# One re-planned kernel: Wq loaded in row halves, halved first-tile chains, doubled VectorE tiles, and 32 short reads of Wqkv on ScalarE's queue

## The chip, the cores and the metric

The kernel runs on one core of one Trainium2 chip. The metric is the device time of the launch in microseconds (us); lower is better. The time before is 184.14 us, the median of three runs (184.11 to 184.27).

## What is computed

One layer block in bf16: a layer norm, then a sliding dilated attention and a gated feed-forward on the same normalised rows, and both are added to the input. S is 2048, D is 512, with 32 heads of 16 values; each position attends to 8 positions, spaced by 2; the hidden width is 1376.

```python
xn = _layernorm(x, axis=-1)
# _A_ref
qkv = (x @ wqkv)                         # 512 -> 3*512
idx = pos[:, None] - off[None, :]        # off = 0, 2, ..., 14
logits = jnp.einsum("bhsd,bhswd->bhsw", q, kg) * scale
attn = _softmax(jnp.where(mask, logits, -1e9), axis=-1)
o = jnp.einsum("bhsw,bhswd->bhsd", attn, vg)   # then o @ wo
# _B_ref
h = _gelu(x @ w_gate) * (x @ w_up)       # then h @ w_down
return x + _A_ref(xn, A_wqkv, A_wo) + _B_ref(xn, B_w_gate, B_w_up, B_w_down)
```

## The kernel before, in words

The 2048 rows are cut into four blocks b = 0..3 of 512 positions, and each block into tiles of 128 rows. Every piece of work is a named task of a small graph (`Graph`, `Task`, `Item`, lines 64 to 382). The task order of each engine is written out by hand in `ORDER` (line 402 on), one list of names for each of TensorE ("pe"), ScalarE ("act"), VectorE ("dve"), GpSimd ("pool") and the DMA queue ("sp"). `schedule` walks these lists only to hand out buffer slots and to find the waits; it has a model of durations (`PARAMS`, `SCHED`, `d_mm`, `d_act`, `d_dve`), which decides which slot a tile gets, and so some of the waits, but does not move a task. An engine works strictly down its list, so a task that waits holds up all that stands behind it.

The stages, with the names that are used below:

- Loads on SP: the first four row tiles (`ld_x0_0` and so on, line 731), Wqkv in three column parts `ld_wq`, `ld_wk`, `ld_wv` (line 687), further row tiles (line 737), then Wg and Wu (`ld_wg0`, `ld_wu0`, line 696), which wait until Wk has landed, and the rest.
- Layer norm: for block 0 on VectorE (`bnst`, `bnag`, `sub`, `rstd`, `norm`; lines 750 to 873) with square roots on ScalarE (`sq`); tile 1 has its sums on ScalarE (`sx1`, `sxx1`, line 760). For later tiles it is on ScalarE. Block 0 is transposed on TensorE (`tpx`, line 899) and evicted by ScalarE and VectorE (`evx`, `evy`); later blocks are transposed by DMA (`trx`, line 882).
- Q, K, V: for block 0, Q and K are made tile by tile (`mma0_0`, `mmt`, line 959: 16 matmuls of 128 columns for each tile), V in four matmul groups of 512 columns (`mm0_2_0_0` to `mm0_2_3_0`, line 1009). For later blocks all twelve groups are 512 wide. ScalarE evicts them (`evq`, `evk`, `evv`, lines 986 and 1020).
- Logits: VectorE multiplies Q by the shifted K for one of four head groups at a time, 4096 elements for each partition (`pr`, line 1040), adds pairs (`pa`, line 1053; a third add only for block 3, `PR_ADD3`), and TensorE sums over the head values with a fixed matrix (`er`, line 1085, 16 matmuls for blocks 0 to 2, 8 for block 3), together with a part of the feed-forward (line 1078).
- Softmax: on VectorE a max over 8 straight from PSUM (`d1`, line 1117), a subtraction in PSUM (`d2`, line 1122), on ScalarE `exp`, then three adds (`d4a` to `d4c`, line 1141), `ln`, `d5`, and the product `d6` (line 1159). The result goes to DRAM (`ss`, line 1168) and comes back replicated to all partitions (`sl`, line 1180).
- Output of attention: VectorE multiplies V by the weights in four parts of 4096 elements (`pv`, line 1188), adds them up (`pw`, line 1197) and folds the sum (`pz`, line 1203).
- Feed-forward: eleven gate and up groups for each block (`fg`, `fu`, lines 1221 and 1260) with gelu and copies on ScalarE (`gelu`, `uev`) and the product on VectorE (`h`, line 1245).
- Down projection and Wo sum in one PSUM tile (`acca`, `accb`, `accd`, `accw`, line 1306); ScalarE evicts (`fe`, line 1339), VectorE adds the input rows (`fin`, lines 1344 and 1350), which were loaded again into XR (`ldxr`, line 1292), and SP stores (line 1357).

TensorE warms up on constants (`warm`, line 678) before the first transpose. PSUM has eight slots in one pool, so TensorE waits for ScalarE where a slot is to be used again.

Of the kernel before, what the change touches and what calls it, by code (L numbers as in the profile page):

```python
# [9 lines left out]
    LAT_X=0.08,  # L10
    LAT_S=0.03,
    TOL=dict(pe=0.6, act=-0.3, dve=0.0, pool=0.0, sp=0.0),
    DMA_ISSUE=0.48,
    DMA_FIXED=2.0,
    DMA_BPUS=330e3,
    ACT_SWITCH=1.35,
    PE_SLACK=0.0,
    PE_MODE_SWITCH=0.115,
    PE_DRAIN=0.2,
    DRAIN=0.1,  # L20
    PE_COLD_F=2.0,
    HAM_TAU=4.0,
    HAM_ENTER=0.52,
    HAM_EXIT=0.30,
)


class PeClock:

    def __init__(self, prm):  # L30
        self.tau = prm["HAM_TAU"]
        self.enter = prm["HAM_ENTER"]
        self.exit = prm["HAM_EXIT"]
        self.f = prm["PE_COLD_F"]
        self.avg = 0.0
        self.t = 0.0
        self.warm = False

    def run(self, start, dur, util):
        import math  # L40
        if start > self.t:
            self.avg *= math.exp(-(start - self.t) / self.tau)
            if self.warm and self.avg < self.exit:
                self.warm = False
            self.t = start
        left = dur
        total = 0.0
        while left > 1e-9:
            step = min(left, 0.2)
            real = step * (1.0 if self.warm else self.f)  # L50
            a = math.exp(-real / self.tau)
            self.avg = self.avg * a + util * (1.0 - a)
            if not self.warm and self.avg > self.enter:
                self.warm = True
            elif self.warm and self.avg < self.exit:
                self.warm = False
            total += real
            left -= step
        self.t = start + total
        return total  # L60

# [36 lines left out]
class Task:  # L98
    def __init__(self, idx, eng, name, dur, emit, prio, table, nbytes, batch, mode=None, latest=None,
# [6 lines left out]
        self.on_act = False  # L106
        self.idx = idx
# [28 lines left out]
class Graph:  # L136
# [70 lines left out]
    def schedule(self, orders, params=None):  # L207
        prm = dict(PARAMS)
        prm.update(params or {})
        LAT_X, LAT_S = prm["LAT_X"], prm["LAT_S"]  # L210
# [12 lines left out]
        efree = dict((e, 0.0) for e in ENGS)  # L223
        act_table = None
        pe_mode = None
        pe_clock = PeClock(prm)
        dma_free = 0.0

        def rdy(t, p, od):
            if p.eng == t.eng and (p.eng == "pe" or od):  # L230
                return p.end
            return p.done + (LAT_S if p.eng == t.eng else LAT_X)

# [33 lines left out]
        for _ in range(len(self.tasks)):  # L267
# [17 lines left out]
            if t.eng == "sp":  # L285
                t.end = est + (t.dur or prm["DMA_ISSUE"])
                t.done = t.end
                if t.nbytes > 0:
                    dma_free = max(t.end, dma_free) + t.nbytes / prm["DMA_BPUS"]
                    t.done = dma_free + prm["DMA_FIXED"]  # L290
            elif t.eng == "pe":
                sw = 0.0
                if t.mode is not None:
                    if pe_mode not in (None, t.mode):
                        sw = prm["PE_MODE_SWITCH"]
                    pe_mode = t.mode
                t.end = est + sw + pe_clock.run(est, t.dur, t.util)
                t.done = t.end + prm["PE_DRAIN"]
            else:
                t.end = est + t.dur  # L300
                t.done = t.end + prm["DRAIN"]
                if t.eng == "act" and t.table is not None:
                    act_table = t.table
# [60 lines left out]
    def emit_engine(self, eng_name, e):  # L364
        if eng_name == "act":
            for t in self.order["sp"]:
                if t.on_act:
                    assert not t.waits
# [20 lines left out]
    def report(self):  # L389
# [16 lines left out]
        "warm0 warm1 warm2 warm3 warm4 warm5 warm6 warm7 warm8 warm9 tpx0_0 warm10 warm11 warm12 warm13 "  # L406
        "warm14 mma0_0 tpx0_1 mmt0_0 mmt0_1 mmt1_0 tpx1_0 mmt1_1 mmt0_2 tpx1_1 mmt1_2 mmt0_3 mmt1_3 "
        "mm0_2_2_0 mm0_2_1_0 fg0_0 mm0_2_0_0 fg0_1 fg0_2 fg0_3 fu0_0 fu0_1 mm0_2_3_0 fg0_4 fu0_2 fu0_3 fu0_4 "
        "fg0_5 mm1_1_0_0 mm1_0_0_0 fu0_5 fg0_6 er0_3 mm1_0_1_0 mm1_1_1_0 fg0_7 mm1_1_3_0 mm1_0_2_0 mm1_2_3_0 "
        "fg1_0 mm1_0_3_0 mm1_1_2_0 fg1_1 fu1_0 fu1_1 fu0_6 fu0_7 fg1_2 fu1_2 mm1_2_2_0 mm1_2_1_0 fg1_3 fu1_3 "  # L410
        "fg0_8 fg1_4 fu0_8 mm1_2_0_0 fg1_5 fg0_9 fu1_4 fu0_9 fu1_5 fg1_6 fg0_10 fu1_6 mm2_0_0_0 mm2_1_0_0 "
        "mm2_1_1_0 mm2_0_2_0 er1_3 fg1_7 mm2_0_3_0 mm2_0_1_0 fg1_8 mm2_1_3_0 mm2_2_0_0 fg2_0 mm2_1_2_0 accd2 "
        "fu1_7 accd1 mm2_2_2_0 fu1_8 acca0 fg1_10 mm2_2_3_0 accb0 fg2_1 fg2_2 accd3 fg2_3 fu2_0 fg1_9 fu2_1 "
        "mm2_2_1_0 fu2_2 fu2_3 er2_3 mm3_1_0_0 mm3_1_3_0 fu1_9 mm3_0_0_0 mm3_1_2_0 mm3_0_2_0 mm3_2_1_0 "
        "mm3_0_1_0 mm3_1_1_0 fg3_0 mm3_0_3_0 fg2_4 mm3_2_0_0 mm3_2_2_0 mm3_2_3_0 fu3_0 fu2_4 fg2_5 fg2_10 "
        "accd7 fu2_5 fg3_1 fu3_1 fg3_2 accd5 acca4 er3_3 fg2_6 accb4 accd6 fu2_6 fg2_7 fg2_8 fg3_10 fu2_7 "
        "fu3_2 fu2_8 fg3_3 fg3_4 fu3_3 fg3_5 fg2_9 fu2_9 fu3_4 fg3_6 fu3_5 fg3_7 fu3_6 fu3_7 fg3_8 fg3_9 "
        "fu3_8 accd11 acca8 accd10 fu3_9 accd9 accb8 acca12 accd13 accd14_0 accd14_1 accw14_0 accw14_1 "
        "accw13 accd15_0 accb12 accw15_0 accw12 accd15_1 accw15_1 accd15_2 accw15_2",
    "act":  # L420
        "c_tbl sx1 sq0 negm1 sxx1 sq1 evx0_0 evx0_1 evq0_0 sq2 evq0_1 evk0_0 evx1_0 sq3 evk0_1 bnst8 evx1_1 "
        "bnst9 evq0_2 evk0_2 evq0_3 evk0_3 ve8 sq6 vp8 sq4 bnag8 evv0_2_0 evv0_1_0 halo1 bnag9 evv0_0_0 va8 "
        "gelu0_0 bnst10 gelu0_2 uev0_0 bnst11 ve10 evv0_3_0 gelu0_1 vp10 gelu0_3 uev0_3 uev0_1 bnag10 "
        "evk1_0_0 evq1_0_0 gelu0_5 bnag11 gelu0_4 uev0_5 uev0_4 uev0_2 vb8 evq1_1_0 evk1_1_0 gelu0_6 gelu0_7 "
        "exp0 sub8 va10 evq1_2_0 vb10 ln0 sub11 d5_0 evk1_3_0 evq1_3_0 evv1_3_0 uev1_0 evk1_2_0 sub9 uev1_1 "
        "uev0_6 uev0_7 gelu1_1 gelu1_0 evv1_1_0 sub10 norm9 uev0_10b gelu1_3 evv1_2_0 gelu0_8 norm10 norm8 "
        "uev1_2 gelu1_2 norm11 gelu1_5 uev1_3 gelu1_4 bnst12 gelu0_9 uev0_9 uev1_5 uev0_8 uev0_10a bnst13 "
        "uev1_6 uev0_10c evv1_0_0 evq2_0_0 gelu0_10 evk2_1_0 ve12 evk2_0_0 vp12 evq2_2_0 bnag12 gelu1_6 "
        "uev1_4 evq2_3_0 gelu1_7 bnag13 evq2_1_0 halo2 evk2_3_0 exp1 bnst14 va12 bnst15 vb12 ve14 evk2_2_0 "
        "vp14 uev1_10b bnag14 ln1 uev1_7 d5_1 sub13 halv1 fe2 bnag15 uev1_8 va14 vb14 sub15 sub12 fe1 "  # L430
        "uev1_10c evv2_2_0 sub14 norm12 norm13 fe0 evv2_3_0 evv2_0_0 gelu2_2 gelu2_1 norm14 fe3 norm15 halo3 "
        "uev1_10a gelu2_0 gelu1_10 uev2_1 evv2_1_0 uev2_0 uev2_3 uev2_2 gelu1_8 uev2_10b uev2_10c gelu2_3 "
        "gelu1_9 evq3_0_0 evk3_0_0 evq3_2_0 evk3_3_0 evk3_2_0 evq3_1_0 exp2 halv2 evk3_1_0 uev1_9 evv3_0_0 "
        "evv3_3_0 ln2 evv3_2_0 evq3_3_0 d5_2 evv3_1_0 uev3_0 halv3 gelu2_5 uev2_10a gelu2_4 uev2_5 uev2_4 "
        "uev3_1 fe5 gelu2_10 gelu3_1 fe7 fe4 uev3_10c gelu3_2 gelu3_0 exp3 uev3_10b uev2_6 uev2_7 fe6 ln3 "
        "uev3_2 d5_3 uev2_8 gelu2_6 uev3_3 gelu2_7 gelu2_9 uev2_9 gelu2_8 gelu3_4 gelu3_5 uev3_5 gelu3_3 "
        "gelu3_6 uev3_6 uev3_4 uev3_7 gelu3_7 fe11 gelu3_10 fe10 gelu3_9 uev3_10a uev3_9 gelu3_8 uev3_8 fe8 "
        "fe9 fe13 fe12",
    "dve":
        "c_wdz bnst0 bnag0 sub0 rstd0 norm0 mean1 sub1 evy0_0 rstd1 norm1 evy0_1 bnst2 bnag2 sub2 rstd2 "  # L440
        "norm2 bnst3 bnag3 sub3 rstd3 norm3 bnst6 bnst4 bnst5 bnst7 bnag6 bnag5 bnag4 bnag7 sub4 sub5 sub6 "
        "sub7 pr0_1 rstd6 rstd4 norm7 norm5 norm6 pr0_0 norm4 pr0_3 pr0_2 pa0_0 pa0_1 pr1_0 mask d1_0 h0_1 "
        "d2_0 pr1_1 h0_2 d4a_0 d4b_0 d4c_0 pa1_0 d6_0 pr1_3 pr1_2 h0_3 rstd8 pa1_1 h0_0 h1_0 rstd10 pv0_1 "
        "pv0_0 pv0_2 pw0_1 h1_1 pv0_3 pw0_2 h0_4 d1_1 pw0_3 d2_1 pz0 h0_10 pr2_0 d4a_1 pr2_1 d4b_1 d4c_1 "
        "pr2_2 d6_1 pr2_3 pa2_0 rstd12 pa2_1 h1_3 fin2 h1_2 pv1_0 rstd14 pv1_2 pv1_3 pv1_1 h1_10 pw1_1 d1_2 "
        "pw1_2 d2_2 pw1_3 pr3_0 d4a_2 pz1 d4b_2 h1_4 d4c_2 pr3_2 pr3_3 fin1 d6_2 pr3_1 h2_0 pa3_0 pa3_1 fin0 "
        "h2_1 pa3_2 pv2_1 d1_3 h2_10 d2_3 fin3 pv2_0 h2_2 d4a_3 pv2_2 d4b_3 h3_0 d4c_3 pw2_1 d6_3 pw2_2 fin7 "
        "pv2_3 h2_3 pw2_3 h2_4 fin6 pz2 pv3_1 pv3_2 fin4 pv3_0 pv3_3 h3_2 fin11 h3_3 fin5 pw3_1 h3_1 h3_10 "
        "h3_4 fin10 pw3_2 fin8 pw3_3 fin9 pz3 fin14_0 fin14_1 fin13 fin15_0 fin15_1 fin12 fin15_2",
# [15 lines left out]
def d_mm(n, cnt=1):  # L465
    return cnt * max(64, n) * 0.4213e-3


def d_act(n):
    return 0.10 + 0.00085 * n  # L470
# [950 lines left out]
```

## Time and profile before, and how to read it

| what | value |
|---|---|
| median of 3 runs | 184.14 us (184.11 to 184.27) |
| profiled execution: span from first to last instruction | 182.8 us |
| median less the span (launch and end, around the instructions) | 1.3 us |
| busy: TensorE, VectorE, ScalarE | 178.0 us (97%), 168.8 us (92%), 129.3 us (71%) |
| mean granted TensorE clock | 0.999 |
| DMA: bytes and share of 16 engines | 19.44 MB, 36.3% |
| first Wg matmul, last matmul's end | 17.17 us, 180.28 us |

The profiled execution's own time is its span and the 1.3 us around it. "PE" is TensorE's matmuls, "PEld" its weight loads, "DVE" VectorE, "ACT" ScalarE, "POOL" GpSimd, "SPq" the queue of DMA issues. A group's line gives busy time, mean ns of one instruction, and the idle time of the engine just before it, with what ended it. Durations of neighbours on one engine overlap in part: four matmuls of 128x512 are recorded with 379 ns each but follow each other 0.86 us for four, and two VectorE products of 4096 elements, recorded with 2287 ns each, take 4.49 us together. For a sum over a chain the distance from start to start is the right measure.

### The profile page before, as it was taken

To read this page: it belongs to the slowest core of one execution; us is meant where nothing else is said; L and a number is where in the kernel's file an instruction comes from. 1 tells how busy PE (TensorE), PEld (TensorE's weight loads), DVE (VectorE), ACT (ScalarE), POOL (GpSimd) and SP (SyncE) were. 2 spreads that over 40 slices of the span, in tenths; PEclk is the share of its full clock that TensorE was granted. 3 is DMA by queue.
4 is the path that set the end of the run, shared out by engine and by line. 5 is a ranking of instruction groups with operands and counts; after the bars stand their busy time and mean duration, and the time that the engine had idled before them with its cause. 6 is when DMAs were issued, how large, how long until landed. Compare 5 with 4: busy or idle time off the path is not lost.

```text
span 182.8 us, 2777 instructions
## 1 busy us (share of the span) xinstructions
PE 178.0 (97%) x1060; PEld 89.8 (49%) x1060; DVE 168.8 (92%) x169; ACT 129.3 (71%) x266; POOL 11.1 (6%) x23
## 2 busy tenths in 40 slices
PE   8799999999999999999999999999999999999994
PEld 2685444554444544444444555444444444444673
DVE  3769999999999999999999989999999999999932
ACT  5589977899899899869997596934396764145011
POOL 6000000104000000504000000000000000000000
PEclk9999999999999999999999999999999999999999
DMA  4999559610364000002742000136310246222333
GB/s 111 359 376 377 132 113 299 211 50 21 97 190 98 0 0 0 4 14 74 201 115 61 0 0 0 37 81 158 129 59 0 46 138 221 57 84 74 91 106 107
DMA packets 26220, 19.60 MB, mean 107 GB/s; under 512 B 13824, under 2 KB 23008, under 8 KB 26208
## 3 DMA queue, kind: packets, MB, share of 16 engines
q1 hardware_dynamic: 26208, 19.44, 36.3%
q8 instruction: 8, 0.13, 0.3%
q14 instruction: 4, 0.03, 0.1%
HBM read 14.71 MB, written 3.15 MB: 98 GB/s over the span
## 4 chain that ended last, share of the span: by engine, by line
PE 89%; DMA 8%; SPq 1%; issue 0%; DVE 0%; DVEq 0%
PE PS L1221 38%; PE PS L1306 28%; PE PS L1009 18%; DMA Wg<-in_B_w_gate_dram 5%; DMA Wqkv<-in_A_wqkv_dram 3%; PE PS L1260 2%; PE PS L1085 2%; PE PS L1078 1%; SPq L731 1%; SPq L687 0%; DVE OB L1350 0%; DVEq L376 0%
## 5 line engine op out<-in xcount | busy, mean ns | idle before, releaser
L1306 PE MATMUL PS<-Wd,HT 128*128 128x512 bf16 (+2 forms) x209 | 40.8, 345 | 0.0
L1221 PE MATMUL PS<-xnT,Wg 128*128 128x512 bf16 x160 | 39.6, 379 | 0.3 <-DMA Wg<-in_B_w_gate_dram 0.3
L1221 PE MATMUL PS<-xnT,Wu 128*128 128x512 bf16 x160 | 38.8, 379 | 0.0
L1009 PE MATMUL PS<-xnT,Wqkv 128*128 128x512 bf16 x160 | 37.8, 379 | 0.0
L1040 DVE TENSOR_TENSOR UNI<-QT,KT 128x4096 f16<-128x4096 bf16 x16 | 36.4, 2287 | 0.1
L1188 DVE TENSOR_TENSOR UNI<-VN,PT 128x4096 f16<-128x4096 bf16 x16 | 36.0, 2286 | 0.0
L1306 PEld LDWEIGHTS PS<-Wd,HT 128*128 128x128 bf16 x209 | 19.7, 98 | 19.0
L1238 ACT ACTIVATE UU<-PS 128x512 bf16<-128x512 f32 x40 | 22.8, 604 | 7.9 <-PE PS L1221 6.2
L1197 DVE TENSOR_TENSOR UNI<-UNI 128x4096 f16<-128x4096 f16 x12 | 27.4, 2286 | 0.0
L1009 PEld LDWEIGHTS PS<-xnT,Wqkv 128*128 128x128 bf16 x160 | 17.9, 114 | 16.9 <-ACT UU L1238 0.4
L1231 ACT ACTIVATE GG<-PS 128x512 bf16<-128x512 f32 x40 | 23.4, 600 | 2.5 <-DVE HT L1245 1.7
L1221 PEld LDWEIGHTS PS<-xnT,Wg 128*128 128x128 bf16 x160 | 15.4, 98 | 19.6 <-DMA Wg<-in_B_w_gate_dram 0.7
L1221 PEld LDWEIGHTS PS<-xnT,Wu 128*128 128x128 bf16 x160 | 15.7, 98 | 18.8
L1339 ACT ACTIVATE OB<-PS 128x512 bf16<-128x512 f32 x14 | 8.2, 594 | 21.8 <-PE PS L1306 21.8
L1053 DVE TENSOR_TENSOR UNI<-UNI 128x4096 f16<-128x4096 f16 x9 | 20.4, 2282 | 0.0
L1306 PE MATMUL PS<-Wo,OT 128*128 128x512 bf16 (+2 forms) x76 | 16.5, 345 | 0.0
L1245 DVE TENSOR_TENSOR HT<-GG,UU 128x1024 bf16<-128x1024 bf16 x20 | 13.6, 686 | 0.0
L832 POOL TENSOR_TENSOR sq<-ve,mhalf 128x2 bf16<-128x2 f32 x4 | 8.2, 2058 | 73.3 <-ACT ve L828 73.3
L1020 ACT ACTIVATE VN<-PS 128x512 bf16<-128x512 f32 x16 | 9.3, 594 | 2.5 <-PE PS L1009 2.5
L1306 PEld LDWEIGHTS PS<-Wo,OT 128*128 128x128 bf16 x76 | 7.2, 98 | 6.5
L1020 ACT ACTIVATE QT<-PS 128x512 bf16<-128x512 f32 x12 | 7.2, 597 | 3.2 <-PE PS L1009 3.2
L959 PE MATMUL PS<-xnT,Wqkv 128*128 128x128 bf16 x128 | 8.2, 219 | 1.2 <-DMA Wqkv<-in_A_wqkv_dram 1.0
(85 smaller groups left out, 153.9 us busy)
## 6 DMA issues: line engine op xcount, KB each, us to landing
PT<-pt_scratch SPq DMA_DIRECT2D x16, 256.0 KB, 4.0
XR<-in_A_x_dram SPq DMA_DIRECT2D x16, 128.0 KB, 2.4
out_dram<-OB SPq DMA_DIRECT2D x14, 128.0 KB, 2.0
Wqkv<-in_A_wqkv_dram SPq DMA_DIRECT2D x3, 512.0 KB, 5.6
XIN<-in_A_x_dram SPq DMA_DIRECT2D x6, 256.0 KB, 6.0
Wg<-in_B_w_gate_dram SPq DMA_DIRECT2D x1, 1280.0 KB, 8.8
Wu<-in_B_w_up_dram SPq DMA_DIRECT2D x1, 1280.0 KB, 11.6
Wd<-in_B_w_down_dram SPq DMA_DIRECT2D x1, 1280.0 KB, 7.7
```

The source lines that it names most:

```text
L832: "pool", "sq%d" % t, 7.0, lambda e, t=t, n=n: e.tensor_tensor(out=sq[:, t:t + n], in0=ve[:, t:t + n], in1=mhalf[:, 0:n], op=ALU.pow),
L1009: ins = e.matmul(PS[:, 512 * it.slot:512 * it.slot + 512], lhsT=wcols(which, kt, g), rhs=xnT[:, itx.slot, kt, :], start=(kt == 0), stop=(k ...
L1020: return e.activation(out=o, in_=PS[:, 512 * it.slot:512 * it.slot + 512], func=ACTF.Identity, scale=(QSC, 1.0, 1.0)[which])
L1040: return lambda e: e.tensor_tensor(out=UNI[:, it.slot, :, :], in0=bass.AP(QT, (itq.slot * 4 + g) * 512, [[NQT * 4 * 512, 128], [0, 8], [1, ...
L1053: return lambda e: e.tensor_tensor(out=UNI[:, i0.slot, :, :], in0=UNI[:, i0.slot, :, :], in1=UNI[:, i1.slot, :, :], op=ALU.add)
L1188: return lambda e: e.tensor_tensor(out=bass.AP(UNI, ito.slot * 4096, [[NUNI * 4096, 128], [2048, 2], [512, 4], [1, 512]]), in0=bass.AP(VN, ...
L1197: return lambda e: e.tensor_tensor(out=UNI[:, i0.slot, :, :], in0=UNI[:, i0.slot, :, :], in1=UNI[:, i1.slot, :, :], op=ALU.add)
L1221: ins = e.matmul(PS[0:M, 512 * it.slot:512 * it.slot + 512], lhsT=Wx[:, kt, j * 128:j * 128 + M], rhs=xnT[:, itx.slot, kt, :], start=(kt = ...
L1231: return lambda e: e.activation(out=GG[:, ito.slot, q, :], in_=PS[:, 512 * it.slot:512 * it.slot + 512], func=ACTF.Gelu_apprx_tanh)
L1238: return lambda e: e.activation(out=UU[:, ito.slot, q, :], in_=PS[:, 512 * it.slot:512 * it.slot + 512], func=ACTF.Identity)
L1245: return lambda e: e.tensor_tensor(out=HT[:, ito.slot, j - 1:j + 1, :], in0=GG[:, ig.slot, :, :], in1=UU[:, iu.slot, :, :], op=ALU.mult)
L1306: ins = e.matmul(PS[:, 512 * it.slot:512 * it.slot + CW], lhsT=(OT[:, ito.slot, q, ti * 128:(ti + 1) * 128] if kind == "o" else HT[:, ith. ...
```

## The change

The two files differ in the schedule lists of all five engines and in these parts of the program:

1. `ld_tch`: a DMA of 32 rows by 32 bf16 values (every 16th row of Wqkv, 64 bytes each) into a tile that nothing reads. It is issued by ScalarE at the head of its list, after a wait for VectorE's first instruction (the memset `c_wdz`).
2. `ld_wq` becomes `ld_wq0` and `ld_wq1`, each with 256 of the 512 rows.
3. For tiles 0 and 1, `norm` is cut into two halves of 256 columns, the transposes into `tpx` and `tpy` with two each, and the Q matmuls into `mma` (8 matmuls on the first row half of Wq) and `mmb` (8 on the second).
4. V of block 0 is made in four groups of 8 matmuls of 256 columns (`mmv0_0` to `mmv1_1`); three of the four now stand ahead of the first Wg group.
5. `pr`, `pa`, `pv` and the first `pw` become instructions of 8192 elements (half as many of them). The third add (`pb`) is now made for blocks 1, 2 and 3, so `er1` and `er2` have 8 matmuls in place of 16.
6. Softmax: ScalarE copies the logits from PSUM to SBUF as bf16 (`lc`, new, 128x1024); the max is three VectorE instructions on that copy (`d1a` 512, `d1b` 256, `d1c` 128 elements), the subtraction works on the copy, and `exp` reads it.
7. The reload of the input rows for blocks 2 and 3 goes into XIN's buffers, not XR's.
8. The planner's model of durations is a new one; it has effect through the slots that it hands out.

```diff
+        t_w = G.task("sp", "ld_tch", 0.01, lambda e: e.dma_start(tch[:, :], A_wqkv[0:512:16, 0:32]),
+                     rd=[(I_wd, 2)], wr=[I_tch])
+        t_w.on_act = True
...
+                        return lambda e: e.dma_start(
+                            Wqkv[:, 2 * h:2 * h + 2, 0:512],
+                            A_wqkv[256 * h:256 * h + 256, 0:512].rearrange("(k p) n -> p k n", p=128))
...
+                        nm = "norm%d%s" % (t, "ab"[h])
+                        t_of[nm] = G.task("dve", nm, 0.15, mk_nm(), rd=[(I_rstd, t)] + ([I_xs] if t else []),
+                                          wr=[(it_x, (t, h))])
...
+                                for g in range(2):
+                                    for kt in range(4):
+                                        c = 512 * it.slot + 256 * g
+                                        ins = e.matmul(PS[:, c:c + 256], lhsT=wcols(2, kt, 2 * gp + g),
+                                                       rhs=xnT[:, itx.slot, kt, 256 * h:256 * h + 256],
+                                                       start=(kt == 0), stop=(kt == 3))
...
-                        in0=bass.AP(QT, (itq.slot * 4 + g) * 512, [[NQT * 4 * 512, 128], [0, 8], [1, 512]]),
+                        in0=bass.AP(QT, (itq.slot * 4 + 2 * h) * 512, [[NQT * 4 * 512, 128], [512, 2], [0, 8], [1, 512]]),
...
-    PR_ADD3 = cfg.get("PR_ADD3", (3,))
+    PR_ADD3 = cfg.get("PR_ADD3", (1, 2, 3))
...
-                return lambda e: e.tensor_reduce(
-                    out=msv(0), in_=lgv(0, 128, [(1, 128), (128, 8)]), axis=AX.X, op=ALU.max)
+                return lambda e: e.activation(out=PB[:, it.slot, :], in_=lgv(0, 128, [(1, 1024)]), func=ACTF.Identity)
+            G.task("act", "lc%d" % b, d_act(1024), mk_lc(), rd=[it_lg], wr=[it_pb])
...
+                    return lambda e: e.tensor_tensor(
+                        out=SUB[:, 0:w], in0=PB[:, it.slot, 0:w] if w == 512 else SUB[:, 0:w],
+                        in1=PB[:, it.slot, w:2 * w] if w == 512 else SUB[:, w:2 * w], op=ALU.max)
```

The head of the lists, before and after (later parts are re-ordered throughout):

```diff
 "pe"
-"... tpx0_0 warm10 ... warm14 mma0_0 tpx0_1 mmt0_0 mmt0_1 mmt1_0 tpx1_0 mmt1_1 mmt0_2 tpx1_1 mmt1_2 mmt0_3 mmt1_3 mm0_2_2_0 mm0_2_1_0 fg0_0 mm0_2_0_0 ..."
+"... tpx0_0 tpy0_0 warm10 ... warm14 mma0_0 tpx0_1 tpy0_1 mmb0_0 mma0_1 mmb0_1 mmt1_0 tpx1_0 mmt1_1 mmt1_2 tpx1_1 mmt0_2 mmv0_1 mmt1_3 mmt0_3 mmv0_0 mmv1_0 fg0_0 ..."
 "dve"
-"... norm3 bnst6 bnst4 bnst5 bnst7 bnag6 bnag5 bnag4 bnag7 sub4 sub5 sub6 sub7 pr0_1 rstd6 rstd4 norm7 norm5 norm6 pr0_0 norm4 ..."
+"... norm3 bnst4 bnst5 bnag4 bnag5 bnst6 bnst7 bnag6 rstd4 sub5 bnag7 sub4 sub7 norm5 rstd6 norm4 sub6 norm7 norm6 pr0_1 pr0_0 pa0 h0_1 mask h0_0 rstd8 d1a_0 ..."
 "sp"
-"ld_x0_0 ld_x0_1 ld_wq ld_x1_0 ld_wk ld_x1_1 ld_wv ld_x2 ld_x4 ld_x3 ld_wg0 ld_wu0 ..."
+"ld_x0_0 ld_x0_1 ld_tch ld_wq0 ld_wq1 ld_x1_0 ld_wk ld_x1_1 ld_wv ld_x2 ld_x4 ld_x3 ld_wg0 ld_wu0 ..."
```

## The prediction, made before the result was known

> **What bounds the kernel now.** I read the page's busy shares first: TensorE 97%, VectorE 92%. A share near 100% says who may be the bound, not where, so next comes the chain of work that ended last, as shares and in order of time.
>
> ```profile
> PE 89%; DMA 8%; SPq 1%; issue 0%; DVE 0%; DVEq 0%
> ...
> 2.75 5.60 DMA Wqkv<-in_A_wqkv_dram
> 8.35 0.02 issue
> 8.37 8.76 DMA Wg<-in_B_w_gate_dram
> 17.13 0.05 issue
> 17.17 1.04 PE PS L1221 x4
> ```
>
> From 17.17 us to 180.28 us the chain holds TensorE alone, 163.11 us without a pause. Ahead of it stand two loads: Wk, whose landing at 8.35 releases Wg's issue, and Wg, which lands at 17.13. So the end is (landing of Wg) + (TensorE's work after it) + a fixed tail. TensorE's own waits confirm it; there are only three in the whole run:
>
> ```profile
> PE PS L959 <- DMA Wqkv<-in_A_wqkv_dram: 1.0, 1, 1.0
> PE PS L678 <- PEq L1406: 0.8, 1, 0.8
> PE PS L1221 <- DMA Wg<-in_B_w_gate_dram: 0.3, 1, 0.3
> ```
>
> The windows of half a microsecond show the loads (columns: stretch, length, busy of PE, PEld, DVE, ACT, POOL, clock, DMA share, GB/s):
>
> ```profile
> 2.50:3.00 0.50, 0.50 (x3) 0.22 (x2) 0.00 (x0) 0.00 (x0) 0.39 (x3) 1.00 1.12 271
> 3.00:3.50 0.50, 0.50 (x3) 0.22 (x2) 0.44 (x1) 0.07 (x1) 0.47 (x2) 1.00 0.67 74
> 3.50:4.00 0.50, 0.50 (x3) 0.15 (x1) 0.43 (x2) 0.50 (x2) 0.33 (x1) 1.00 0.81 135
> 4.00:4.50 0.50, 0.50 (x2) 0.15 (x1) 0.48 (x2) 0.47 (x5) 0.00 (x0) 1.00 0.88 227
> ...
> 6.00:6.50 0.50, 0.00 (x0) 0.00 (x0) 0.19 (x1) 0.00 (x0) 0.00 (x0) 1.00 1.10 389
> ```
>
> The rate falls to 74 GB/s when Wqkv's first bytes are due, with the engines occupied, and recovers by 5 us; later parts of the same matrix, with the same rows, run at 380. From 3.0 to 4.5 the stream moves 218 KB where 380 GB/s would move 570: a hole of 0.93 us ahead of Wg. Last, VectorE: its timeline shows one unbroken run from the first logits product at 16.48 to the end of `pz3` at 173.34. It is nearly a second bound.
>
> ```profile
> 172.12 1.22 DVE L1203 TENSOR_TENSOR OT<-UNI 128x2048 bf16<-128x2048 f16 x1
> ...
> 173.76 1.90 PE L1306 MATMUL PS<-Wo,OT 128*128 128x256 bf16 x12
> ```
>
> The second line is `accw14_0`, the first to need `pz3`: 0.4 us later. ScalarE has much to spare after 100 us (the windows give 15.0 of 20 us, then 10.3), but is busy 54.7 of the 60 us from 20 to 80.
>
> **What the Trainium skill says.** "TensorE: Matmul & The Clock Gate", section "Wait — 56ns, not 53.3ns?": a warm matmul costs columns / 2.4 GHz + 2.5 ns, 215.8 for 512. The trace agrees: four take 0.863. So 256-column matmuls for V cost 109 each, no more per column. "VectorE: DVE Perf Modes", section "Side-by-side: where the cycles go": some 150 cycles per instruction beside the elements. Recorded, the trace agrees (1221 ns for 2048, 2286 for 4096: 156 + 0.520 each), but in a run of products only 2.20 us lie from start to start, so joining two saves 0.07. "DMA: Bandwidth & Descriptors", section "Issuing engines are not separate DMA queues": a DMA from ScalarE runs on the same 16 engines, so the short reads share, not bypass, the stream; no trace yet shows two issuers.
>
> **The change, part by part.**
>
> *TensorE after Wg.* Two V groups (1.73 us) stood behind `fg0_0`, now one (0.87): -0.86. `er1` and `er2` lose 8 matmuls each, 0.43 by the chain's rows for 16 (0.86) and 8 (0.43): -0.86. All else is the same work in another order: 163.11 - 1.72 = 161.39.
>
> *Wg's landing.* The same 4.2 MB lie ahead of its end. The short reads carry 2 KB, so bytes cost nothing. If the hole at 3 us is a first-access cost of Wqkv, they pay it from about 1.7 (memset ends 1.18, issue 0.45) while x still streams; if not, they gain nothing, and can disturb x by about one issue, 0.2. Bounds: -0.93 to +0.2. Against it, the added SP issue (0.43 to 0.5 a piece) puts Wk's issue from 2.75 to 3.2, and Wk releases Wg; with the queue full this is hidden, uncovered it costs 0.45. Taken: -0.4, the middle of a recovered hole. Wg lands at 16.7.
>
> *TensorE before Wg.* From Wq's landing at 6.65 to 16.92 there are 9.8 us of work and 0.5 of pauses; the third V group adds 0.87. Now Wq's first half is half the bytes: 262 KB of x and 262 KB make 524 KB, which the windows reach at 4.6; landings trail the byte count by 0.5 to 1.25 us, so 5.1 to 5.9. The halved norm and transposes save about 0.15 on the way to `mma0_0`, which was done 0.75 before Wq anyway. The start at 5.9 gives 5.9 + 10.67 + 0.2 = 16.8: as late as Wg. `fg0_0` at 16.8. The matmul end: 16.8 + 161.4 = 178.2 against 180.28: -2.1.
>
> *ScalarE at the start.* The touch waits for VectorE (1.18) and takes 0.45; behind it stand the table load (1.28) and one activation, finished near 3.2, before tile 1 is there at 3.43. Hidden by 0.2 us; if not, 0.2 on tile 1's chain.
>
> *VectorE.* Two more adds +4.4; 24 joined pairs -1.7; `d1` 1.13 against 0.36 + 0.22 + 0.15, four times, -1.6; `d2` 1.13 against 0.60, -2.1: net -1.0. Norms of tiles 4 to 7 (1.3 us) move ahead of the first product; they fill the 1.10 us in which VectorE waited for x, since tile 4 is now first. First product at 16.2. Against that, a new stall: `mask` waits for `er0`, `lc0` for `mask`, `d1a_0` for `lc0`, with only `h0_0` between: about 2.1 us more, and 0.7 at `d6_0`, where `ln0` stands behind five ScalarE tasks. Start 16.2 + 152.5 of work + 2.8 + 0.6 of small waits = `pz3` done at 172.1. `accw13`, now the first to need it, has 5.3 us of TensorE behind its start: due at 172.9. Margin 0.8. `accd3` on `pz0` is closer: due 74.7, ready 74.4.
>
> *ScalarE.* Four copies at 1.0 us (by the exp row, 1023 ns from the same PSUM tile). Added by start-to-start times, its work ahead of each reused PSUM slot stands 2.2 to 3 us before TensorE's use, where it was 4.3 to 6. `lc0` waits about 1.9 us for `er0`, with nine evictions queued behind it up to `ln0`; TensorE waits for those. The cushion is half eaten, not gone. The last V group of block 0 comes at 51 us, its eviction at about 52.4; `pv0_1` is due at 53.6.
>
> *SP.* The four `trx` for block 1 move from 19.26 to about 16.4, as all norms are done; queued behind Wu they land near 23, needed at 24.6. `ss` and `sl` keep 8 us against a need of 9. `ldxr` in XIN waits on tiles long used. Hidden.
>
> *Sum.* 184.14 stands for 182.8 + 1.34. -2.1 for TensorE, +0.1 for small waits: 182.1.
>
> **Rivals.**
> - *The short reads do nothing.* Wg lands at 17.13 to 17.2 (the hole belongs to the row pattern or the first big queue). For: later Wqkv parts are already under way when the rate recovers. Then only -1.72 + 0.1: 182.5.
> - *VectorE becomes the bound.* Another 1.0 us of stall at `lc`, or `sl` later than thought, and `accd3` and `accw13` wait. Against: the later `lc` have other work between. -2.1 + 1.0: 183.1.
> - *ScalarE becomes the bound: slower.* Place: 20 to 80 us. 54.7 busy + 2.0 for two copies + 4.0 waiting at `lc0` and `lc1` + its old 5.3 of idle make 66 in 60. Of the 6 over, 3 are cushion; TensorE pauses 3.0 for PSUM slots: 184.14 - 2.1 + 3.0 = 185.0. It decides once ScalarE's lag exceeds about 2.2 us. Against it: much of the old idle is waiting for TensorE, which vanishes as it falls behind.
>
> **How the numbers follow.** The likeliest case 0.50 (its own range 181.3 to 182.7), useless reads 0.17, VectorE 0.18, ScalarE 0.11, a mixture within the bound 0.04. 0.2% is 0.37 us, about what a measurement of this kernel can tell from no change. Faster: 0.50 + 0.17 + 0.18 = 0.85; same 0.04; slower 0.11. The range runs from full recovery of the hole and TensorE following it (another -0.5 and rounding, 181.2) to the VectorE case with more stall (183.8); outside lie the ScalarE case and some of each end.
>
> **What would show it.** Right: the half-microsecond windows from 3 to 4.5 no longer fall below 200 GB/s; `mma0_0` before 6.0; Wg's first matmul at 16.4 to 17.0; TensorE about 161.4 us from there to the end; `er1` at 0.43. Wrong: pauses of TensorE between 20 and 80 with ScalarE evictions as releaser, at `accd3` or at `accw13` with `pz0` or `pz3`; the copy `lc` well over 1.0 us; a joined product well over 4.4 us; transposes landing after 24.6.

## The result: no change that can be measured, and the profile after

The changed kernel takes 184.11 us (median of 14 runs, 183.74 to 185.23) against 184.16 us before (14 runs, 183.93 to 184.42). The ratio is 0.9999, with a 95% interval of 0.9989 to 1.0009. The forecast was 182.1.

TensorE still ends the run, but the chain of waits has another shape. Here it is after the change, the shares by engine and then the pieces in order of time (start, length, what):

```profile
PE 59%; ACT 23%; DVE 6%; POOL 5%; DMA 3%; issue 2%; SPq 1%; DVEq 0%
...
3.21 5.81 DMA Wqkv<-in_A_wqkv_dram
9.02 0.05 issue
9.06 1.08 PE PS L962 x16
...
15.94 1.75 PE PS L1020 x16
17.68 7.77 PE PS L1265 x36
```

Two things differ. Wg (line 1265 now) no longer stands in the chain as a transfer: TensorE reaches it only after a run of its own work that begins with Wk's landing at 9.02. And from 32 to 94 us the chain leaves TensorE, for ScalarE, GpSimd and VectorE. The head of TensorE in its timeline:

```profile
5.60 0.64 PE L976 MATMUL PS<-xnT,Wqkv 128*128 128x128 bf16 x8
6.30 0.48 PE L898 MATMUL PS<-ident,XIN 128*128 128x128 bf16 x4
6.62 1.53 PE L976 MATMUL PS<-xnT,Wqkv 128*128 128x128 bf16 x24
9.06 1.08 PE L962 MATMUL PS<-xnT,Wqkv 128*128 128x128 bf16 x16 [0.92 <-DMA Wqkv<-in_A_wqkv_dram]
...
17.52 1.03 PE L1265 MATMUL PS<-xnT,Wg 128*128 128x512 bf16 x4
```

The first Q matmul begins at 5.60, a microsecond earlier than in the profile before. Not all of this comes from the halves of Wq: with Wq whole and the rest of the change (e7, below) it begins at 5.96. Then TensorE stands for 0.92 us in front of the first K matmul. From there to the first Wg matmul, 8.46 us, it does not pause. The windows of half a microsecond show what the loads do (stretch, length, busy of PE, PEld, DVE, ACT, POOL, clock, DMA share, GB/s):

```profile
3.00:3.50 0.50, 0.50 (x3) 0.22 (x2) 0.50 (x1) 0.29 (x2) 0.45 (x2) 1.00 0.41 72
3.50:4.00 0.50, 0.50 (x3) 0.15 (x1) 0.43 (x3) 0.50 (x3) 0.35 (x1) 1.00 1.05 324
...
5.00:5.50 0.50, 0.50 (x9) 0.40 (x7) 0.47 (x3) 0.50 (x4) 0.00 (x0) 1.00 0.92 260
5.50:6.00 0.50, 0.50 (x9) 0.41 (x8) 0.35 (x3) 0.23 (x2) 0.00 (x0) 1.00 0.81 199
6.00:6.50 0.50, 0.43 (x8) 0.20 (x5) 0.44 (x2) 0.00 (x0) 0.00 (x0) 1.00 0.80 264
```

The hole at 3.0 is still there (72 GB/s, 74 before). It closes sooner, but a second, shallower one follows: 199 to 264 GB/s between 5 and 6.5 us, where the kernel before had 389 at 6.0. That is where Wk goes late.

TensorE's waits in the whole run are again few, and the wait for Wg is gone from them:

```profile
PE PS L962 <- DMA Wqkv<-in_A_wqkv_dram: 0.9, 1, 0.9
PE PS L639 <- PEq L1457: 0.8, 1, 0.8
PE PS L898 <- DVE XIN L857: 0.3, 1, 0.3
PE PS L1112 <- ACT UU L1282: 0.2, 1, 0.2
```

Behind the first Wg matmul TensorE now pauses. Before the change there was no pause after 17.17. Three pauses make up 0.75 us, counted from start to start of the matmuls: 0.25 at 48.69, 0.3 at the logits sum of block 2 (94.45) and 0.2 at the output of attention of block 2 (153.49). The chain shows what the second one waits for, and the third is a wait of TensorE's weight loads (us in all, times, longest):

```profile
91.41 0.09 DVE rstd L780
...
91.52 1.33 ACT XIN L830 x2
...
93.33 0.98 ACT UU L1282 x2
...
94.45 0.62 PE PS L1112 x16
```

```profile
PEld PS L1357 <- DVE OT L1247: 0.5, 1, 0.5
```

At the logits sum the last to come was a ScalarE copy, done at 94.30; VectorE's add for this sum had ended at 93.67. ScalarE was late because two norms ahead of the copy had stood 1.62 us for `rstd` on VectorE. At the output TensorE waited for VectorE's `pz` itself, and at 48.69 for a ScalarE copy. At the end of the run VectorE finishes `pz3` at 173.95, 0.6 later than in the profile before:

```profile
172.73 1.22 DVE L1247 TENSOR_TENSOR OT<-UNI 128x2048 bf16<-128x2048 f16 x1
```

### The profile page after: what moved, and what is told of

It reads as the page before. It is cut to its first block, busy times and chain, and to the rows that moved or that the text cites. A ratio compares the mean times of both kernels' runs of the same rounds, so it can differ in the third digit from the quotient of the medians.

```text
span 182.0 us, 2781 instructions
## 1 busy us (share of the span) xinstructions
PE 177.2 (97%) x1060; PEld 90.5 (50%) x1060; DVE 169.1 (93%) x157; ACT 131.8 (72%) x270; POOL 17.9 (10%) x23
## 4 chain that ended last, share of the span: by engine, by line
PE 59%; ACT 23%; DVE 6%; POOL 5%; DMA 3%; issue 2%; SPq 1%; DVEq 0%
PE PS L1357 23%; PE PS L1265 21%; PE PS L1045 9%; POOL sq L809 5%; ACT UU L1282 4%; ACT GG L1275 4%; DMA Wqkv<-in_A_wqkv_dram 3%; PE PS L962 3%; DVE UNI L1076 2%; ACT XIN L830 2%; DVE UNI L1088 2%; PE PS L1020 1%; ACT L1170 1%; ACT EX L1171 1%; ACT PB L1148 1%
## 5 line engine op out<-in xcount | busy, mean ns | idle before, releaser
L1265 PE MATMUL PS<-xnT,Wu 128*128 128x512 bf16 x160 | 39.4, 379 | 0.0
L1227 DVE TENSOR_TENSOR UNI<-VN,PT 128x8192 f16<-128x8192 bf16 x8 | 35.4, 4421 | 0.0
L1076 DVE TENSOR_TENSOR UNI<-QT,KT 128x8192 f16<-128x8192 bf16 x8 | 35.3, 4420 | 0.0
L1045 PE MATMUL PS<-xnT,Wqkv 128*128 128x512 bf16 x144 | 34.7, 379 | 0.1
L1045 PEld LDWEIGHTS PS<-xnT,Wqkv 128*128 128x128 bf16 x144 | 16.1, 113 | 15.7 <-ACT UT L1320 0.6
L809 POOL TENSOR_TENSOR sq<-ve,mhalf 128x2 bf16<-128x2 f32 x4 | 15.1, 3767 | 67.1 <-ACT ve L805 67.1
L1236 DVE TENSOR_TENSOR UNI<-UNI 128x8192 f16<-128x8192 f16 x4 | 17.7, 4421 | 0.0
L1088 DVE TENSOR_TENSOR UNI<-UNI 128x8192 f16<-128x8192 f16 x4 | 17.7, 4420 | 0.0
L1242 DVE TENSOR_TENSOR UNI<-UNI 128x4096 f16<-128x4096 f16 x4 | 9.1, 2287 | 0.0
L1056 ACT ACTIVATE KT<-PS 128x512 bf16<-128x512 f32 x12 | 7.2, 601 | 2.0 <-PE PS L1045 2.0
L1056 ACT ACTIVATE VN<-PS 128x512 bf16<-128x512 f32 x12 | 7.2, 598 | 1.0 <-PE PS L1045 0.9
```

The costliest lines, as they stand in the source:

```text
L809: "pool", "sq%d" % t, 5.0, lambda e, t=t, n=n: e.tensor_tensor(out=sq[:, t:t + n], in0=ve[:, t:t + n], in1=mhalf[:, 0:n], op=ALU.pow),
L1045: ins = e.matmul(PS[:, 512 * it.slot:512 * it.slot + 512], lhsT=wcols(which, kt, g), rhs=xnT[:, itx.slot, kt, :], start=(kt == 0), stop=(k ...
L1056: return e.activation(out=o, in_=PS[:, 512 * it.slot:512 * it.slot + 512], func=ACTF.Identity, scale=(QSC, 1.0, 1.0)[which])
L1076: return lambda e: e.tensor_tensor(out=UNI[:, it.slot:it.slot + 2, :, :], in0=bass.AP(QT, (itq.slot * 4 + 2 * h) * 512, [[NQT * 4 * 512, 1 ...
L1088: return lambda e: e.tensor_tensor(out=UNI[:, i0.slot:i0.slot + 2, :, :], in0=UNI[:, i0.slot:i0.slot + 2, :, :], in1=UNI[:, i1.slot:i1.slo ...
L1227: return lambda e: e.tensor_tensor(out=bass.AP(UNI, ito.slot * 4096, [[NUNI * 4096, 128], [2048, 4], [512, 4], [1, 512]]), in0=bass.AP(VN, ...
```

## The experiments

All runs but e5 were timed in five rounds beside the kernel before on the same chip. A ratio is to that kernel before, with a 95% interval; none of the differences reaches 1%, and those whose interval leaves out 1 are clear of the scatter. Where a load lands is read from one profiled execution of each kernel. "Wk lands" is read from the issue of Wg, which waits for it. Line numbers are those of each kernel.

### What the reads are worth, alone and on the other queue: e1, e2, e3

e1 is the changed kernel without the reads:

```diff
-        t_w = G.task("sp", "ld_tch", 0.01, lambda e: e.dma_start(tch[:, :], A_wqkv[0:512:16, 0:32]),
-                     rd=[(I_wd, 2)], wr=[I_tch])
-        t_w.on_act = True
```

> The changed kernel without the 32 short reads, so ScalarE issues no DMA at all. Theory A (a DMA from a second queue costs about 0.8 us outside the span, since the profiled execution spends 184.13 - 182.0 = 2.1 us around its span where the kernel before had 184.14 - 182.8 = 1.3): time less span falls from 2.1 to 1.3. In the head the hole in the load stream at 3 to 4.5 us returns; whether Wk lands later than 9.02 then decides the rest: 183.3 if the head stays as it is, 184.0 if the reads were worth what they cost. Rival B (the 0.8 us around the span is scatter, and the reads do save time in the head): time less span stays near 2 or is near 1.3 for both, and the span grows by 0.5 to 0.9, so 184.6 to 185.0.

e2 is the kernel before with these lines added, and with ScalarE's queue made to wait for the memset; in e3, the changed kernel, the read goes to SP's queue and waits for nothing:

```diff
-                     rd=[(I_wd, 2)], wr=[I_tch])
-        t_w.on_act = True
+                     wr=[I_tch])
```

> The kernel before with the 32 short reads alone, on ScalarE's queue, held until VectorE's first memset. Theory A: time less span rises from 1.3 to 2.1; Wqkv's landing and Wg's first matmul move earlier by up to 0.5; in all 184.1 to 184.9. Rival B: no such rise, and the first Wg matmul moves from 17.17 to about 16.7: 183.7.

> The changed kernel with the same short reads issued by SP, third in its list (where the list names them), so that no second queue is in use; every later load is issued about 0.45 us later. Theory A: time less span is back at 1.3; the span grows by the later issue, 0 to 0.5: 183.3 to 183.9. Rival B: time less span stays as in the changed kernel, 184.1 to 184.6.

Measured: e1 184.13 us, ratio 1.0000 (0.9985 to 1.0015); e2 184.23, ratio 0.9998 (0.9981 to 1.0014); e3 184.39, ratio 1.0012 (1.0002 to 1.0022). The reads on ScalarE's queue are worth nothing, with or without the rest of the change. In e2 they landed 1.9 us after their issue at 1.21, and the hole stood at 102 and 70 GB/s from 3 to 4 us all the same; so 32 short reads, of every 16th row of Wqkv, did not pay for it in advance. They landed only as the hole began: what reads that are done earlier would do is not shown. On SP, one issue later for everything, they put Wk's landing at 9.18. The other theory, that a DMA from a second queue costs 0.8 us outside the span, failed as well: 2.09 us lie around the span without the reads in e1, and 1.91 with them in e2.

### Wq in one load again: e4, and without the reads: e7

```diff
-                for h in range(2):
-                    def mk(h=h):
-                        return lambda e: e.dma_start(
-                            Wqkv[:, 2 * h:2 * h + 2, 0:512],
-                            A_wqkv[256 * h:256 * h + 256, 0:512].rearrange("(k p) n -> p k n", p=128))
-                    t_w = G.task("sp", "ld_wq%d" % h, 0, mk(), wr=[(I_wq, ("q", h))], ...)
+                t_w = G.task("sp", "ld_wq0", 0, mk(), wr=[(I_wq, ("q", 0)), (I_wq, ("q", 1))], ...)
```

> The changed kernel with Wq in one load again; halved chains, short reads and all else kept; the first Q matmuls wait for all of Wq. If the added SP issue (0.45 us) is what makes Wk land at 9.02 where it landed at 8.35, Wk lands at about 8.5, the TensorE pause of 0.9 us before the first K matmuls shrinks to 0.4, and the time falls by 0.3 to 0.5 to 183.7. If the load stream itself is slow from 4.5 to 8 us (200 to 313 GB/s, where it was 324 to 389), Wk lands near 9.0 all the same and the first Q matmuls start later than 5.60: 184.1 to 184.4.

> The changed kernel with Wq in one load and without the short reads. Theory (the reads are worth nothing): 183.3, as with the reads and Wq in one load (183.27). Rival (the reads do recover part of the hole, and it was hidden by the halves in the earlier pair): 183.6 to 183.8.

Measured: e4 183.27 us, ratio 0.9960 (0.9944 to 0.9976), more than the 0.3 to 0.5 us that was expected; e7 183.28, ratio 0.9951 (0.9939 to 0.9963). This is the version that beats both kernels, by 0.4 to 0.5%, and again the reads make no difference. Against the changed kernel 0.84 us are won by leaving Wq whole. In e7 the issue of Wg and TensorE's head read:

```profile
7.72 0.37 SPq L661 DMA_DIRECT2D Wg<-in_B_w_gate_dram  x1
```

```profile
14.89 1.91 PE L1011 MATMUL PS<-xnT,Wqkv 128*128 128x256 bf16 x16
16.64 1.67 PE L1256 MATMUL PS<-xnT,Wg 128*128 128x512 bf16 x7
```

Wk lands at 7.70, 1.3 us earlier than in the changed kernel, TensorE never waits for it, and the first Wg matmul starts 0.88 earlier (17.52 to 16.64). From the first K matmul to it are 8.46 us in both kernels (8.18 to 16.64 here), so the whole difference lies ahead of K. The time follows nearly one for one.

### Was the profile before typical? e5

> The kernel before, unchanged, profiled a second time. Theory: the profile that the prediction was built on caught an execution some 0.6 us slower than the median, all of it in the head's loads; the span is then about 182.2 us, Wq lands near 5.9 instead of 6.65, the first Wg matmul starts at 16.5 to 16.8 instead of 17.17, TensorE's work after it is again 163.1 us, and the time around the span is about 1.9 us, not 1.3. Rival: the first profile was typical and the head is 17.2 again.

```profile
2.75 5.21 DMA Wqkv<-in_A_wqkv_dram
7.98 8.66 DMA Wg<-in_B_w_gate_dram
16.69 1.04 PE PS L1221 x4
```

It was not typical. The same kernel, profiled again, has a span of 182.3 us and took 184.16 us itself. Everything up to Wg comes 0.4 to 0.5 us earlier than in the chain that the forecast was built on (8.37 and 17.17 there), and TensorE's work after it is the same: from 16.69 to 179.79, 163.10 us. One point of the expectation failed: the first Q matmul came at 6.52, not 5.9, behind VectorE's norm, which cost nothing. The 43 timed runs of the kernel before beside e1 to e4 have a median span of 182.3, and 1.92 us around it on average, not 1.34. The 184.14 of the forecast's sum and the span of 182.8 did not belong to the same execution.

### The cut alone, in the kernel before: e6 by rows, e9 by columns, e8 on Wk

e6 gives the kernel before the two row halves of the change and nothing else; e9 cuts by columns instead; e8 is the changed kernel with Wq whole and Wk cut:

```diff
+                            Wqkv[:, 2 * h:2 * h + 2, 0:512],        # e6
+                            Wqkv[:, :, 256 * h:256 * h + 256],      # e9
+                            Wqkv[:, 2 * h:2 * h + 2, 512:1024],     # e8
```

> The kernel before with one edit: Wq in two row halves. Theory (the halves slow the loads that follow them): Wk lands about 0.7 us later than in the kernel before (at 8.6 to 9.0), Wg is issued and lands that much later, the first Wg matmul starts at 17.3 or later, and the time is 184.9 to 185.1. Rival (the halves cost only 0.45 us of issue, hidden in a full queue; the slow stream comes from something else in the change): 184.2 to 184.3.

> The kernel before with Wq in two column halves (256 of 512 columns, all 512 rows each) instead of two row halves. Theory A (the rate falls when a load first reaches rows of Wqkv that no load has read): one hole only, from 3 to 4 us, no second one from 5 to 6.5; Wk lands near 8.1, the first Wg matmul starts at 16.7 to 16.9, 184.1 to 184.3. Theory B (a split of the first weight load costs, whatever its rows): a second hole below 200 GB/s between 5 and 6.5 as with row halves (119 and 172), first Wg matmul at 17.3, about 184.85.

> The changed kernel with Wq in one load and Wk in two row halves. Theory (any early load that is cut into halves slows the stream behind it): Wk's last half lands at 8.7 to 9.0 instead of 8.25, TensorE waits for it, 183.8 to 184.1. Rival (only a split of the first Wqkv load costs, since the second half then meets the slow first accesses): 183.2 to 183.5.

Measured: e6 184.85 us, ratio 1.0033 (1.0021 to 1.0046); e9 184.93, ratio 1.0060 (1.0045 to 1.0075); e8 183.43, ratio 0.9964 (0.9954 to 0.9973). The cut of Wq is slower by itself. In e6 Wk lands at 8.72 instead of 7.96, as the issue of Wg shows:

```profile
8.74 0.37 SPq L705 DMA_DIRECT2D Wg<-in_B_w_gate_dram  x1
```

Its windows, of the same columns as above:

```profile
3.00:3.50 0.50, 0.50 (x3) 0.22 (x2) 0.50 (x1) 0.03 (x1) 0.47 (x2) 1.00 0.62 147
4.00:4.50 0.50, 0.50 (x3) 0.10 (x1) 0.32 (x2) 0.47 (x4) 0.00 (x0) 1.00 1.04 367
5.00:5.50 0.50, 0.47 (x9) 0.48 (x9) 0.42 (x3) 0.47 (x3) 0.00 (x0) 1.00 0.43 119
5.50:6.00 0.50, 0.24 (x5) 0.07 (x3) 0.47 (x3) 0.42 (x2) 0.00 (x0) 1.00 0.74 172
```

The first hole closes sooner than in e5 (365 GB/s from 3.5 to 4, against 102), and then the stream falls to 119 GB/s. Cut by columns, so that the first half reaches every row, the second hole is the same (125, 170, 164 from 5 to 6.5 us): theory A of e9, that a load pays for rows which no load has read yet, is out for the second hole. With Wk cut in place of Wq there is no second hole (367, 375 and 367 GB/s over the same stretch), and the cost against e4 is within 0.16 us.

### What joins the cut and Wk's landing: e12, e13, e15, e16, e14

e12 adds an issue but no cut (the kernel before, with the reads on SP behind Wq), e13 keeps the cut but issues Wk on time:

```diff
-"ld_x0_0 ld_x0_1 ld_wq ld_x1_0 ld_wk ..."
+"ld_x0_0 ld_x0_1 ld_wq ld_tch ld_x1_0 ld_wk ..."          # e12
+"ld_x0_0 ld_x0_1 ld_wq0 ld_wq1 ld_wk ld_x1_0 ..."         # e13
```

> The kernel before with Wq in one load and one more issue on SP: the 32 short reads, 2 KB in all, between Wq and the third row tile. Theory C (the head is set by the time of issue: Wk lands 5.0 to 5.5 us after its issue, and each issue ahead of it costs 0.45 us or more): Wk is issued at 3.2 and lands at 8.4 to 8.8 instead of 7.96, first Wg matmul at 17.1 to 17.3, 184.6 to 184.9. Theory B (only a split of Wq costs): Wk lands at 8.0 in spite of the later issue, 184.1 to 184.3.

> The kernel before with Wq in two row halves and Wk issued ahead of the third row tile, so at 2.7 as in the kernel before. Theory C: no hole in front of Wk; Wk lands at 7.5 to 8.0, Wg is issued before 8.0; the third row tile comes later, and TensorE may wait for it, so the time itself can be anything from 184.0 to 185.5. Theory B (the second hole follows from the split itself): a hole below 200 GB/s between 5 and 6.5 again, Wk at 8.4 or later.

Measured: e12 184.58 us, ratio 1.0027 (1.0013 to 1.0042); e13 184.86, ratio 1.0039 (1.0021 to 1.0057). In e12 a load of 2 KB puts Wk 0.68 us later. The queue of SP:

```profile
3.20 0.44 SPq L691 DMA_DIRECT2D Wqkv<-in_A_wqkv_dram  x1
...
8.66 0.37 SPq L700 DMA_DIRECT2D Wg<-in_B_w_gate_dram  x1
```

Theory C (the time of issue) holds there, and theory B (only a cut) falls. In e13 it is the other way round: Wk was issued at 2.72, and landed at 8.54 through a hole of 186 GB/s at 5.0 to 5.5.

e15 and e16 tried to make both one: Wk, in halves as well, can begin sooner. e15 is e1 with that edit, e16 is e6 with it (the line of e8 above, beside the halves of Wq).

> The changed kernel without the reads, with Wq in two row halves as in the change and Wk in two row halves as well. Theory D (the queue runs dry: a load's first bytes come about 1.3 us after its issue ends if it has 256 KB and about 1.9 us if it has 512 KB, so with Wq in halves the stream is through with all that was issued before whole Wk, issued late, can begin): Wk's first half begins near 5.0, there is no gap at 5 to 6.5, Wk lands at 7.6 to 8.0 instead of 8.77, the first Wg matmul starts at 16.3 to 16.8, 182.9 to 183.3. Theory B (a cut of Wq costs, whatever follows): the gap is there, Wk lands at 8.5 or later, 184.0 to 184.5.

> The kernel before with Wq and Wk in two row halves each. Theory D: no gap at 5 to 6.5; Wk lands at 7.6 to 8.0 instead of 8.72 with Wq alone in halves, the first Wg matmul starts at 16.3 to 16.8, 183.9 to 184.2. Theory B: the gap is there, Wk at 8.6 or later, 184.8 to 185.2.

Measured: e15 184.03 us, ratio 1.0002 (0.9988 to 1.0016); e16 184.74, ratio 1.0036 (1.0021 to 1.0051). In e15 Wk landed at 7.79 and no window between 4 and 8.5 us fell below 293 GB/s, as theory D (the queue runs dry) wanted; but ScalarE then waited for a later row tile until 12.39, TensorE stood 0.53 us for ScalarE, and the first Wg matmul came at 17.21. In e16 the hole stayed (158 GB/s from 5.5 to 6) and Wk landed at 8.52. One for, one against: the dry queue is not shown to be the cause.

e14 takes an issue away from SP (e7 with `t_x.on_act = True` for the second row tile).

> The changed kernel without the reads and with Wq in one load, and with the second row tile issued on ScalarE's queue instead of SP's, so that every issue on SP behind it comes 0.45 us earlier. Theory C: Wq is issued at 1.27 and lands at 5.4 to 5.6, Wk is issued at 2.3 and lands at 7.2 to 7.4, first Wg matmul at 16.3 to 16.4 instead of 16.8, 182.8 to 182.9. Rival (the bytes of x and Wqkv set the pace, not the issue): Wq and Wk land as before, 183.2 to 183.3.

Measured: 183.60 us, ratio 0.9977 (0.9969 to 0.9985), so 0.3 slower than e7. All issues on SP came 0.45 earlier, and Wk landed at 7.88, no sooner than in e7 (7.70). Earlier issue gained nothing at Wk, and the first row tile, now sharing the stream, came later: VectorE's first statistics began at 3.53 (2.89 in e7). The first Wg matmul started near 16.96, 0.32 later than in e7, which is the loss in time. (The trace has it at 17.18, but one matmul record is missing there: the V groups ahead of it begin at 15.21, and in e7 they take 1.75 us to the first Wg matmul.)

What is shown: in the kernel before, one more DMA issue ahead of Wk, with 2 KB in it or with half of Wq, goes with a Wk that lands 0.68 to 0.76 us later (e12, e6) and costs 0.5 to 0.7 us of the time; an issue fewer does not give it back. The number of issues is not the whole of it: in e13 no more of them stand ahead of Wk than in the kernel before, and it lands 0.58 us later; in e15, where Wk is cut too, one more stands ahead of its first half, and it is on time. A landing is read from a single execution, and two of the kernel before differ by 0.39 us; but the profiles fall apart in two groups. With Wq in one load and no read on SP, Wk lands at 7.57 to 7.96 in eight of nine; with Wq cut, at 8.52 to 9.18 in seven of eight, e15 being the exception. Why a second hole opens is left open. In the packet records of e6 and e12 most packets of 1024 bytes take 46 ns inside the hole as outside it; single ones take 0.2 to 0.8 us, and in parts of it fewer engines are at work. That says how it looks, not what causes it.

### VectorE, the joined products and GpSimd: e10 and e11

In the changed kernel one GpSimd instruction, the first `sq` of block 3, on two values for each partition, took 8.29 us (2.74 before), and it stands in the chain of waits. e10 moves VectorE's wait for it ahead of a joined product, e11 issues each joined instruction as two of 4096 elements; both are edits of e7.

```diff
-"... d4c_1 pr2_0 rstd12 d6_1 ..."
+"... d4c_1 rstd12 pr2_0 d6_1 ..."                          # e10
...
-                    return lambda e: e.tensor_tensor(
-                        out=UNI[:, it.slot:it.slot + 2, :, :],
+                    return lambda e: [e.tensor_tensor(      # e11, likewise in pa, pv and pw
+                        out=UNI[:, it.slot + k, :, :],
...
+                        op=ALU.mult) for k in range(2)][-1]
```

> The changed kernel without the reads and with Wq in one load, and with one name moved in VectorE's list: the reciprocal that waits for GpSimd's sq of block 3's first pair stands ahead of the product before it. Theory (GpSimd's pow cannot end while VectorE runs one long product after another, and ends some 0.6 us after VectorE falls idle): sq starts at 71.1 and ends near 75.1, 4 us long instead of 8.3, VectorE waits 0.6 us as before, and the time is 183.1 to 183.4. Rival (the pow is that slow by itself): it ends at 79.4 again, VectorE waits 4.9 us, and the time is 185 or more.

> The changed kernel without the reads and with Wq in one load, and with each joined VectorE instruction of 8192 elements issued as two of 4096. Theory (VectorE is now close to being the bound, and joining was worth 0.07 us for each of 24 pairs): 1.7 us more VectorE work, the pause at the output of attention grows from 0.2 to over 1 us, 183.9 to 184.6. Rival (the long instructions cost more than they save, since they hold GpSimd up): sq is at most 4.5 us long, the pause of TensorE at the logits sum of block 2 is gone, 182.9 to 183.3.

Measured: e10 183.28 us, ratio 0.9969 (0.9959 to 0.9979), the same as e7; e11 184.04, ratio 1.0010 (0.9993 to 1.0028), 0.76 us slower than e7. GpSimd's timeline in e7, and then in e10:

```profile
71.14 8.30 POOL L800 TENSOR_TENSOR sq<-ve,mhalf 128x2 bf16<-128x2 f32 x1 [38.42 <-ACT ve L796]
```

```profile
71.13 3.96 POOL L800 TENSOR_TENSOR sq<-ve,mhalf 128x2 bf16<-128x2 f32 x1 [38.44 <-ACT ve L796]
```

It starts at the same moment and ends when VectorE lets go: in both, 0.58 us after VectorE has nothing more to do but wait for it. This agrees with the Trainium skill, "SBUF — State Buffer", section "Who interferes with whom": a VectorE instruction with two SBUF inputs contends with a GpSimd instruction that reads SBUF, for ports that only one of them can hold at a time. Here, in e7, it was held through five VectorE instructions one behind the other, each with two SBUF inputs; in e5 a `sq` beside a VectorE reduction from PSUM took 0.71 us. The length of each instruction did not matter: in e11, with products half as long, `sq` took 8.57 us. Not every such instruction keeps it out: `sq` of block 2 in the changed kernel ended at 30.52, 0.57 us after the add that held it, while VectorE's next product of two SBUF tiles (29.87 to 30.55) still ran. What makes the difference is not settled.

The long `sq` costs no time either way. e10 freed it 4.3 us earlier, and TensorE's pause at the logits sum stayed: from the matmul before to the first of the sum are 0.59 us in e7, and as much in e10 when the one matmul record that its trace lacks there is taken off. There TensorE waits for ScalarE's copy, and ScalarE waited 1.62 us for the `rstd` of VectorE in e10 as in the changed kernel. So the joining was right, and VectorE is the engine behind two of the three pauses. With its 1.6 us more of busy time in e11 (170.4 against 168.8), these two grew by 0.4 and 0.5 us (0.2 of the 0.9 in the first line is a missing matmul record):

```profile
PE PS L1103 <- ACT UU L1273: 0.9, 1, 0.9
...
PE PS L1348 <- DVE OT L1238: 0.5, 1, 0.5
```

## Why the prediction was wrong, step by step

Its error is 2.0 us. It can be laid out along the sum that it made, against the profiled execution of the changed kernel (184.13 us, span 182.0):

| term | forecast | found | error |
|---|---|---|---|
| first Wg matmul | 16.8 | 17.52 | +0.7 |
| TensorE from there to its last matmul | 161.4 + 0.1 | 161.4 + 0.75 | +0.65 |
| from the last matmul to the end of the span | 2.5 | 2.35 | -0.15 |
| around the span | 1.34 | 2.13 | +0.8 |

- *TensorE after Wg: right.* 163.11 - 1.72 = 161.39 was the work; 162.16 us less 0.75 of pauses is what the trace shows. The V group and the shorter `er1` and `er2` are worth what was said.
- *"TensorE before Wg": wrong, and the main step.* The forecast let TensorE run from Wq's first half to Wg with 0.2 us of pauses. Wk came into it only as what releases Wg; whether Wk would be there when TensorE reaches the K matmuls was not asked, although its own quoted chain had Wk as the piece ahead of Wg. The first Q matmul did come earlier (5.60, forecast 5.9). But Wk landed at 9.02 instead of 7.96 to 8.35, TensorE stood 0.92 us for it, and everything behind it moved with it. e6 shows the loss in the kernel before, e4 and e7 its end when Wq is whole: the first Wg matmul is then at 16.6 in both (the trace of e4 has 16.81, with one record missing), 0.2 earlier than forecast. The 10.67 us of work were right: in e7 it is 10.68 from the first Q matmul to the first Wg matmul.
- *"With the queue full this is hidden, uncovered it costs 0.45": the wrong side was taken, and the price was too low.* With an extra issue Wk lands 0.68 to 0.76 us later (e12, e6), and with the cut alone, as many issues ahead as before, 0.58 (e13). The cause of this delay stays open.
- *Wg's landing: right number by luck.* Issued at 9.04, 0.67 later than before, it took 7.7 us where it had taken 8.8, and landed near 16.7, as said. But the -0.4 from the reads does not exist (e2, and e4 against e7). The rival "the short reads do nothing" was right in its mechanism.
- *"184.14 stands for 182.8 + 1.34": wrong, 0.55 us.* A span of one execution was set against the median of others. With e5 as the base, Wg's first matmul before the change is at 16.69, so that a start at 16.8 is no gain at all, and the sum promises half a microsecond less. The other 0.2 is new: the changed kernel has 2.11 us around its span in 14 runs, 1.92 before. It is not the reads (2.09 without them in e1, 1.91 with them in e2). e11 has 1.74; what sets it is not settled.
- *Small waits, 0.1: they were 0.75.* VectorE began its products at 16.73, not 16.2, and `pz3` ended at 173.95, not 172.1. Its idle time between them, 3.3 us, was as forecast (2.8 and 0.6); its work was 153.9 us, not 152.5. (The run of before that the forecast called unbroken had 1.2 us of idle time.) Both rivals, VectorE and ScalarE, hold a little: about 0.5 us of pauses at the logits sum and the output of attention, where VectorE is late, and 0.25 at 48.69, where a ScalarE copy ended TensorE's idle time. The 3.0 us of the ScalarE case did not come, though ScalarE was busy 59.3 of the 60 us from 20 to 80, where it had been 54.7. `lc` took 1.03 us and a joined product 4.42, as forecast.

Where did the gain go? Against e5, the typical execution before, TensorE's stretch after Wg is 0.94 us shorter (163.10 to 162.16: 1.72 less work, 0.75 more pauses). The later start gives 0.83 of it back (16.69 to 17.52), and the tail and the time around the span about cancel (-0.15 and +0.2). With Wq in one load the start is as early as before, and 0.9 us remain: that is e7.

## What to carry to other kernels

When a load is cut so that its first part comes sooner, follow every load behind it to the one that the next stage waits for; here the cut of 512 KB brought the first Q matmul 0.36 us forward (5.96 in e7 to 5.60), made Wk land 1.3 us later, and so cost more than it gave. Before a sum is made on a profile, set its span beside the spans of other runs: a head that was half a microsecond late in that one execution looks like something to be won. And take the second-busiest engine's pauses at their measured price: taking 1.7 us of TensorE's work away let VectorE at 93% show through with 0.5 us, and ScalarE with 0.25.

## What was not expected of the hardware

- An added DMA of 2 KB ahead in the queue went with a 512 KB load that landed 0.68 us later (one profile each; the median of 22 runs was 0.5 us longer), more than the 0.45 us of its issue; taking one issue of 0.45 us off the queue brought that load no earlier (7.88 against 7.70).
- Two loads of 256 KB in place of one of 512 KB opened a second hole in the stream, 119 to 172 GB/s for a microsecond in the kernel before, by rows and by columns alike; the same cut on the next load alone did not, and with both loads cut the hole was there in one kernel (e16) and not in the other (e15).
- A GpSimd instruction on 128x2 values, 0.71 us long in e5 at 33.8 us, took 8.3 us beside five VectorE instructions, each with two SBUF inputs, that followed each other without a gap.
